# Retention with a convolution-gated unit: two float32 buffers behind those of the first two double chunks, value weights loaded later, first gated units held back a phase

## The chip, the core and the metric

The kernel runs on one core of a Trainium2 chip. The metric is the device time of a run in microseconds (us). One execution of the kernel was also recorded by the hardware profiler; its page and its trace are what the readings below come from. Engines are called as in the profile: PE is the matmul engine and PEld its weight loads, DVE, ACT and POOL are the vector, scalar and GpSimd engines, SP is the engine whose queue issues most DMAs.

## The reference

Inputs are q, k and v of shape (8 batches, 8 heads, 576 tokens, 64), and three weights: `w_val` (512 x 512), `conv_w` (5 x 512) and `w_out` (512 x 512). All are float32.

```python
scores = q @ k.T / sqrt(64)
gamma  = 1 - 2 ** (-5 - head)
D      = where(i >= j, gamma ** (i - j), 0)         # per head
x      = (scores * D) @ v                           # heads side by side: (8, 576, 512)
gate   = sigmoid(sum_k conv_w[k] * x[t - 4 + k])    # causal, per channel
out    = (gate * (x @ w_val)) @ w_out               # float32 (8, 576, 512)
```

## The kernel before

The 576 tokens of a batch are cut into two "double chunks" of 256 tokens and a tail of 64. The tails of four batches make one double chunk together. So there are 18 double chunks, m = 0 to 17; m = 8 and m = 17 are the tails. A double chunk has 0.5 MB each of q, k and v.

For one double chunk the work is as follows. SP loads q, k and v as float32 into tiles `fq`, `fk` and `fv` (`load`, L87; for a tail four smaller DMAs each, L92). POOL casts k and q to bf16 (`cast_k`, `cast_q`, L225) and multiplies v by powers of gamma (`cast_v`, L241). PE transposes k and q (`turn(0, m)` and `turn(1, m)`, L263), and ACT copies the result out of PSUM to `kq` (`take_turned`, L271). PE makes the scores (`scores`), DVE masks them (`masks`, L294), and PE multiplies by v (`values`, L308). A running state per batch carries what earlier chunks contribute: PE adds to it (`update`), ACT copies it out (`take_state`, L378), and PE applies it (`carried`). DVE scales the result into the bf16 tile x (`take_x`, L343), and POOL copies the last four tokens to the next chunk's tile (`pass_on`, L356).

The gated unit of a double chunk follows a turn later. The convolution is 40 matmuls with diagonal weights `dg` (`conv`), made on the chip from `conv_w` by `prep_conv_weights` and `prep_diagonals`. ACT applies the sigmoid (`gate`, L407). PE multiplies x by the value weights `wvb`, and DVE multiplies by the gate (`value`, L414 and L417; two calls, i = 0 and 1). Another turn later PE multiplies by the output weights `wob`, ACT copies the result to a tile `ob`, and SP stores it (`project`, L424, L432, L434; two calls).

The value weights arrive as float32 (`wvf`, L112) and are cast to `wvb` in two parts by `prep_wv` (L216), one part on POOL and one on ACT; `value(n, 1)` reads the part of POOL and `value(n, 0)` that of ACT. The output weights arrive as bf16 through POOL's own DMA queue (`load_wo`, L127).

The order is written out by hand: each engine executes its instructions in program order, and so does each queue. A prologue deals with m = 0 and begins m = 1 and 2. The main loop then takes m = 1 to 18. Turn m holds the scores and values of m, the convolution of m-1, `value` of m-1, `project` of m-2, the transposes of m+1, and the casts of m+2. `keep_warm` issues matmuls on zeros.

Tiles come from pools with a fixed number of buffers. The float32 tiles have LB = 4 buffers per kind, so a load of m waits until the cast of m-4 has read its buffer. `ob` has five buffers, so an eviction waits until the output five earlier has been stored. PSUM has two spare banks (`g`) that the convolution, `value` and `project` share.

SP issues the loads in this order: m = 0 and 1, the value weights, m = 2 and 3. In the prologue m = 4, 5 and 6 follow. In the main loop the load of m+6 stands in the middle of turn m, directly after each cast of m+2, between the two outputs of that turn:

```python
            if ok(m + 2):
                for (name, f) in (("k", cast_k), ("q", cast_q), ("v", cast_v)):
                    f(m + 2)
                    if ok(m + 2 + LB):
                        load(name, m + 2 + LB)
```

Of the kernel before, what the change touches and what calls it, by code (L numbers as in the profile page):

```python
# [13 lines left out]
F32 = mybir.dt.float32  # L14
# [7 lines left out]
def kernel(  # L22
# [23 lines left out]
    LB = 4  # L46
# [33 lines left out]
    with tc.manual_schedule():  # L80
# [14 lines left out]
        def load(name, m):  # L95
            t = ld.tile([P, H, R, D], F32, name=f"f{name}")
            fetch(nc.sync, t, {"q": q, "k": k, "v": v}[name], m)
            loaded[name, m] = t
# [3 lines left out]
        for m in range(2):  # L102
            for name in "kqv":
                load(name, m)
# [3 lines left out]
        wv_dst = wvf.rearrange("p (op ob) n -> ob p op n", ob=2)  # L108

        def load_wv(eng, i):  # L110
            for ob in range(2):
                eng.dma_start(out=wv_dst[ob, half[i]], in_=wv_src[ob, i ^ ob])  # L112

        for i in range(2):
            load_wv(nc.sync, i)
        for m in range(2, LB):
            for name in "kqv":
                load(name, m)


        ORDER = ((0, 0, 1, 0), (HP, 0, 0, 1), (0, 2, 0, 0), (HP, 2, 1, 1))
        wob = consts.tile([P, NP, DM], BF16, name="wob")

        def load_wo():
            src = moe_w_out.rearrange("(pr ab hl p) n -> ab hl p pr n", pr=2, ab=2, hl=2)
            for (p0, blk, ab, hl) in ORDER:
                nc.gpsimd.dma_start(out=wob[p0:p0 + HP, blk:blk + 2, :], in_=src[ab, hl])  # L127
# [9 lines left out]
        nc.vector.tensor_tensor(idb, ident[:, 0:HP], ident[:, HP:P], op=ALU.add)  # L137
        toki = consts.tile([P, NCH + 1, R], mybir.dt.int32, name="toki")
# [47 lines left out]
        identf = consts.tile([32, 32], F32, name="identf")  # L186
        nc.vector.tensor_copy(identf, ident[0:32, 0:32])
        id2 = consts.tile([P, HP], F32, name="id2")
        nc.vector.tensor_copy(id2, idb)
# [200 lines left out]
        def conv(n):  # L390

            g = [ps_g.tile([P, 2, 2 * P], F32, name="g") for _ in range(2)][::-1]
            gps[n] = g
            gsb[n] = {}
            lists = [], []
            for pr in range(2):
                a, b = 2 * pr, 2 * pr + 1
                for kk in range(KC):
                    for bank, rows, blks in ((0, half[1], (b, a)), (1, half[0], (a, b))):
# [44 lines left out]
        def keep_warm(n):  # L444

            t = ps_o.tile([P, NP, R, HP], F32, name="o0").rearrange("p o r n -> p (o r n)")
            for _ in range(n):
                nc.tensor.matmul(t, zeros[:, 0:P], zeros, start=True, stop=True)


        keep_warm(8)
        cast_k(0, (v_copy, 4))
        bank = turn(0, 0)
        take_turned(0, 0, bank, (v_copy, 4))
        cast_q(0)
        prep_conv_weights()
        prep_diagonals(0, nc.vector)
# [7 lines left out]
        for m in range(LB, LB + 2):  # L465
            for name in "kqv":
                load(name, m)
        prep_wv(g_copy, 1)
        keep_warm(3)
# [8 lines left out]
        take_state(0, 0)  # L478
        keep_warm(1)
# [3 lines left out]
        prep_diagonals(1, nc.vector)  # L483
        prep_diagonals(2, nc.vector)
        bank = turn(0, 1)
        take_turned(0, 1, bank)
        bank = turn(1, 1)
# [18 lines left out]
        for m in range(1, ND + 1):  # L506
# [43 lines left out]
            if m == 1:  # L550
                prep_wv(s_copy, 0)
                value(0, 1)
# [22 lines left out]
            value(m - 1, 0)  # L575
            if m > 1:
                project(m - 2, 1)
# [31 lines left out]
```

## Time and profile before

| | |
|---|---|
| median of 7 runs | 171.41 us (169.49 to 175.1) |
| the profiled execution | 170.14 us, span 168.4 us, so 1.74 us outside the span |
| mean granted PE clock | 0.961 |
| PE busy | 145.6 us, 86% of the span |
| PEld busy | 107.5 us, 64% |
| DVE busy | 101.0 us, 60% |
| ACT busy | 91.5 us, 54% |
| POOL busy | 77.3 us, 46% |
| DMA | 39.81 MB, mean 236 GB/s |

The span runs from the first to the last instruction. Busy time is the sum of an engine's instructions; it is an average over stages that can have different limits. The page cuts the span in 40 equal slices of 4.21 us and gives a digit for each (9 is 90% busy or more); the row GB/s gives what the DMA engines moved in each slice. A line of waits names the waiting engine, tile and line, then what ended the wait, the total in us, how often, and the longest. A line of a timeline gives start, length, engine, line, operation and count. A stretch line gives the limits, the length, busy times with the number of instructions, the granted clock, the DMA share and GB/s.

### The profile page before, as it was taken

Reading aid. Unit: us, or ns where it says so; the run is one execution under the profiler, and the core shown is the slowest. Engines: PE = TensorE matmul, PEld = TensorE weight load, DVE = VectorE, ACT = ScalarE, POOL = GpSimd, SP = SyncE. Lnnn points to the kernel's source line nnn. Section 1 sums busy time; section 2 is a strip of 40 time slices with the busy share of each in tenths; the row PEclk is TensorE's granted clock in tenths of the full one; section 3 lists DMA queues with packets and bytes.
Section 4 is the critical chain, followed back from the end, with each engine's and each line's share of the span. In section 5 each row is a group of like instructions: output and inputs, shape, how many; then the busy total and the mean of one; then the engine's idle time right before and its main releaser. Section 6 shows DMA issues by size and latency. Waiting matters only on the chain.

```text
span 168.4 us, 7599 instructions
## 1 busy us (share of the span) xinstructions
PE 145.6 (86%) x3344; PEld 107.5 (64%) x3378; DVE 101.0 (60%) x189; ACT 91.5 (54%) x149; POOL 77.3 (46%) x87
## 2 busy tenths in 40 slices
PE   7776888689994939999979999999999999999870
PEld 2355777457672836777757677777778677776620
DVE  6586356457574443677447676676777677667221
ACT  4773655356572514766546575657666575652340
POOL 4384597787749054081970264463828260000000
PEclk9998589999999996999999999999999999999996
DMA  4999999999996789999999999999787111131134
GB/s 132 347 343 222 317 283 260 324 303 323 269 301 159 161 230 298 281 345 312 335 315 344 304 318 308 348 298 272 166 204 264 68 70 62 66 126 64 66 125 125
DMA packets 69055, 39.81 MB, mean 236 GB/s; under 512 B 14219, under 2 KB 63903, under 8 KB 69023
## 3 DMA queue, kind: packets, MB, share of 16 engines
q1 hardware_dynamic: 68256, 38.54, 77.7%
q0 software_dynamic: 576, 0.52, 1.9%
q8 instruction: 26, 0.43, 1.1%
q10 hardware_dynamic: 190, 0.27, 0.6%
q14 instruction: 7, 0.05, 0.1%
HBM read 30.42 MB, written 9.44 MB: 237 GB/s over the span
## 4 chain that ended last, share of the span: by engine, by line
PE 56%; DMA 16%; SPq 10%; POOL 8%; issue 5%; ACT 2%; DVE 1%; ACTq 0%; POOLq 0%
PE g L424 14%; PE g L414 13%; PE g L253 10%; DMA fv<-in_v_dram 9%; PE tps L263 7%; PE o L308 6%; DMA fq<-in_q_dram 5%; PE s L253 4%; SPq L87 4%; SPq L92 4%; POOL vb L241 3%; SPq L112 2%; PE st L253 2%; POOL kb L225 2%; DMA out_dram<-ob 2%
## 5 line engine op out<-in xcount | busy, mean ns | idle before, releaser
L294 DVE TENSOR_TENSOR p<-s,mask 128x512 bf16<-128x512 f32 x62 | 39.9, 686 | 25.2 <-PE s L253 25.1
L271 ACT COPY kq<-tps 128x1024 bf16<-128x1024 bf16 x34 | 34.6, 1018 | 13.1 <-PE tps L263 12.8
L424 PE MATMUL g<-wob,z 128*128 128x512 bf16 x111 | 35.4, 385 | 5.9 <-ACT ob L432 2.7
L432 ACT COPY ob<-g 128x512 f32<-128x512 f32 x34 | 19.9, 586 | 33.8 <-PE g L424 24.8
L241 POOL TENSOR_TENSOR vb<-fv,gin 128x1024 bf16<-128x1024 f32 x18 | 34.3, 1907 | 5.5 <-DMA fv<-in_v_dram 5.5
L414 PE MATMUL g<-x,wvb 128*128 128x256 bf16 x272 | 36.1, 277 | 0.2 <-ACT gate L407 0.2
L253 PE MATMUL g<-x,dg 64*64 64x256 bf16 x720 | 32.3, 282 | 3.7 <-ACT ob L432 2.8
L343 DVE TENSOR_TENSOR x<-o,gout 128x512 bf16<-128x512 f32 x32 | 22.1, 745 | 13.8 <-PE o L308 13.8
L414 PEld LDWEIGHTS <-wvb 128*128 128x128 bf16 x288 | 26.9, 99 | 3.5 <-issue 0.6
L417 DVE TENSOR_TENSOR z<-gate,g 128x512 bf16<-128x512 f32 x34 | 23.4, 687 | 9.0 <-PE g L414 8.0
L356 POOL COPY x<-x 128x16 bf16<-128x16 bf16 x16 | 3.2, 198 | 55.6 <-DVE x L343 55.6
L253 PEld LDWEIGHTS <-dg 64*64 64x64 bf16 x720 | 24.2, 110 | 6.6 <-issue 5.5
L407 ACT ACTIVATE gate<-g 128x512 f32<-128x512 f32 x36 | 21.3, 603 | 10.9 <-PE g L253 5.7
L424 PEld LDWEIGHTS <-z 128*128 128x128 bf16 x144 | 14.1, 98 | 14.6 <-issue 3.4
L225 POOL CAST qb<-fq 128x1024 bf16<-128x1024 f32 x18 | 18.8, 1044 | 5.0 <-DMA fq<-in_q_dram 4.9
L225 POOL CAST kb<-fk 128x1024 bf16<-128x1024 f32 x17 | 17.7, 1044 | 1.5 <-DMA fk<-in_k_dram 1.2
L253 PEld LDWEIGHTS <-kq 64*64 64x64 bf16 x576 | 12.0, 109 | 8.2 <-issue 8.2
L253 PE MATMUL s<-kq 64*64 64x128 bf16 (+1 forms) x560 | 16.5, 222 | 0.8 <-ACT kq L271 0.6
L253 PE MATMUL st<-vb,kb 64*64 64x64 bf16 x512 | 14.3, 197 | 1.6 <-ACT sd L378 1.3
L253 PEld LDWEIGHTS <-kb 64*64 64x64 bf16 x512 | 13.0, 113 | 3.1 <-issue 2.8
L378 ACT CAST sd<-st 128x256 bf16<-128x256 f32 x24 | 8.9, 370 | 9.2 <-PE g L253 6.6
L308 PEld LDWEIGHTS <-vb 64*64 64x64 bf16 x576 | 8.3, 107 | 7.0 <-issue 6.8
(67 smaller groups left out, 113.4 us busy)
## 6 DMA issues: line engine op xcount, KB each, us to landing
fk<-in_k_dram SPq DMA_DIRECT2D x16, 512.0 KB, 6.1
fq<-in_q_dram SPq DMA_DIRECT2D x16, 512.0 KB, 6.4
fv<-in_v_dram SPq DMA_DIRECT2D x16, 512.0 KB, 7.1
out_dram<-ob SPq DMA_DIRECT2D x32, 256.0 KB, 4.2
wvf<-in_moe_w_val_dram SPq DMA_DIRECT2D x4, 256.0 KB, 6.2
fk<-in_k_dram SPq DMA_DIRECT2D x8, 128.0 KB, 4.7
fq<-in_q_dram SPq DMA_DIRECT2D x8, 128.0 KB, 3.9
fv<-in_v_dram SPq DMA_DIRECT2D x8, 128.0 KB, 3.6
```

Source lines behind the costliest of these rows:

```text
L225: copy(t[:, o:o + n], src[:, o:o + n])
L241: eng.tensor_tensor(vbf[m][:, h:h + n], loaded["v", m][:, h:h + n], g[:, h:h + n].unsqueeze(3).to_broadcast([P, n, R, D]), op=ALU.mult)
L253: return lambda: nc.tensor.matmul(*a, skip_group_check=True, **kw)
L271: copy(kq[m][:, which, o:o + n], bank[:, o:o + n])
L294: nc.vector.tensor_tensor(p[:, :, 0:n], sps[m, r][i][:, :, 0:n], mask[dcs[m][0], r].unsqueeze(1).to_broadcast([P, NP, n]), op=ALU.mult)
L308: nc.tensor.matmul(o, start=key not in opened, stop=False, skip_group_check=True, **kw)
L343: nc.vector.tensor_tensor(xg[b // GB][c][:, b % GB, :, x0:x0 + P].rearrange("p o (n r) -> p o r n", r=R), ops[m, ab], gout[:, :, t0:t0 + P ...
L407: nc.scalar.activation(t, gps[n][i], AF.Sigmoid)
L414: nc.tensor.matmul(vps[:, j, :], lhsT=wvb[:, o, 2 * i + j, :], rhs=xs(n, slice(0, P), o, PAD), start=(j == 0 and o == 0), stop=(j == 1 and ...
L417: nc.vector.tensor_tensor(z, gsb[n][i], vps, op=ALU.mult)
L424: nc.tensor.matmul(o, lhsT=zsb[n, j // 2][:, j % 2, i * P:(i + 1) * P], rhs=wob[:, j, :], start=(j == 0), stop=(j == NP - 1))
L432: nc.scalar.copy(ob, o)
```

## The change

The float32 tiles get two sets of buffers: one of two buffers per kind that only m = 0 and 1 use (`fke`, `fqe`, `fve`), and one of two buffers per kind that m = 2 to 17 share. The total of four per kind stays. SP now loads m = 0, 1 and 2 first, then three quarters of the value weights in two DMAs, then m = 3; the last quarter is issued by ACT, between two state copies of the prologue. The load of m = 4 follows the casts of m = 2. In the main loop the load of m+4 stands at the end of turn m, behind the outputs of that turn.

The convolution weights are prepared at the very beginning, two of the four diagonals on POOL, the other two on DVE. The cast of the value weights on POOL and the load of the output weights come after the casts of m = 2; the output weights take three DMAs instead of four. Turn 1 has no `value`; turn 2 has the four of m = 0 and 1, with ACT's weight cast ahead of them; turn 3 has the two of m = 2 and the four projections of m = 0 and 1. From turn 4 on the order of gated units is as it was. Warming matmuls are placed anew. In the weights the order of the half blocks in a tile changes (`ORDER`, and the blocks that `conv` names).

```diff
-    LB = 4
+    LB = 2
...
-            t = ld.tile([P, H, R, D], F32, name=f"f{name}")
+            t = ld.tile([P, H, R, D], F32, name=f"f{name}" + ("e" if m < 2 else ""))
...
-        for m in range(2):
+        for m in range(3):
             for name in "kqv":
                 load(name, m)
...
-        def load_wv(eng, i):
-            for ob in range(2):
-                eng.dma_start(out=wv_dst[ob, half[i]], in_=wv_src[ob, i ^ ob])
-
-        for i in range(2):
-            load_wv(nc.sync, i)
-        for m in range(2, LB):
-            for name in "kqv":
-                load(name, m)
+        nc.sync.dma_start(out=wv_dst[0], in_=moe_w_val.rearrange("(op ob p) n -> ob p op n", ob=2, p=P)[0])
+        nc.sync.dma_start(out=wv_dst[1, half[0]], in_=wv_src[1, 1])
+
+        def load_wv_rest():
+            nc.scalar.dma_start(out=wv_dst[1, half[1]], in_=wv_src[1, 0])
+
+        for name in "kqv":
+            load(name, 3)
...
-            for (p0, blk, ab, hl) in ORDER:
-                nc.gpsimd.dma_start(out=wob[p0:p0 + HP, blk:blk + 2, :], in_=src[ab, hl])
+            nc.gpsimd.dma_start(out=wob[:, 0:2, :], in_=src[HP:HP + P])
+            for pr in range(2):
+                nc.gpsimd.dma_start(out=wob[:, 2 + pr, :], in_=src[:, pr].rearrange("(t p) m -> t p m", p=HP)[0::3])
...
-        keep_warm(8)
+        keep_warm(4)
+        prep_conv_weights()
+        keep_warm(4)
         cast_k(0, (v_copy, 4))
+        for o in range(2):
+            prep_diagonals(o, nc.gpsimd)
         bank = turn(0, 0)
         take_turned(0, 0, bank, (v_copy, 4))
         cast_q(0)
-        prep_conv_weights()
-        prep_diagonals(0, nc.vector)
+        prep_diagonals(2, nc.vector)
+        prep_diagonals(3, nc.vector)
...
-        for m in range(LB, LB + 2):
-            for name in "kqv":
-                load(name, m)
-        prep_wv(g_copy, 1)
-        keep_warm(3)
+        keep_warm(2)
...
         take_state(0, 0)
+        load_wv_rest()
         keep_warm(1)
...
-        prep_diagonals(1, nc.vector)
-        prep_diagonals(2, nc.vector)
         bank = turn(0, 1)
         take_turned(0, 1, bank)
+        keep_warm(2, spare(ps_g, "g"))
...
-        for (name, f) in (("k", cast_k), ("q", cast_q)):
+        keep_warm(4, spare(ps_g, "g"))
+        for (name, f) in (("k", cast_k), ("q", cast_q), ("v", cast_v)):
             f(2)
             load(name, LB + 2)
+        prep_wv(g_copy, 1)
         load_wo()
-        cast_v(2)
-        load("v", LB + 2)
-        prep_diagonals(3, nc.vector)
...
-            if m == 1:
-                prep_wv(s_copy, 0)
-                value(0, 1)
             if nxt:
                 bank = turn(0, m + 1)
                 take_turned(0, m + 1, bank)
-            if m > 1:
-                value(m - 1, 1)
-                project(m - 2, 0)
+
+            if m == 2:
+                prep_wv(s_copy, 0)
+            for (f, n, i) in {1: (), 2: ((value, 0, 1), (value, 0, 0)),
+                              3: ((value, 2, 1), (project, 0, 0), (project, 0, 1))}.get(
+                                  m, ((value, m - 1, 1), (project, m - 2, 0))):
+                f(n, i)
             if ok(m + 2):
-                for (name, f) in (("k", cast_k), ("q", cast_q), ("v", cast_v)):
-                    f(m + 2)
-                    if ok(m + 2 + LB):
-                        load(name, m + 2 + LB)
+                cast_k(m + 2)
+                cast_q(m + 2)
+                cast_v(m + 2)
...
-            value(m - 1, 0)
-            if m > 1:
-                project(m - 2, 1)
+            for (f, n, i) in {1: (), 2: ((value, 1, 1), (value, 1, 0)),
+                              3: ((value, 2, 0), (project, 1, 0), (project, 1, 1))}.get(
+                                  m, ((value, m - 1, 0), (project, m - 2, 1))):
+                f(n, i)
+            for name in "kqv":
+                if ok(m + 2 + LB):
+                    load(name, m + 2 + LB)
```

More of the change, by code (lines that the diff above doesn't have):

```diff
@@ L108 @@
         wv_dst = wvf.rearrange("p (op ob) n -> ob p op n", ob=2)
-        def load_wv(eng, i):
-            for ob in range(2):
-                eng.dma_start(out=wv_dst[ob, half[i]], in_=wv_src[ob, i ^ ob])
-        for i in range(2):
-            load_wv(nc.sync, i)
-        for m in range(2, LB):
-            for name in "kqv":
-                load(name, m)
-        ORDER = ((0, 0, 1, 0), (HP, 0, 0, 1), (0, 2, 0, 0), (HP, 2, 1, 1))
+        nc.sync.dma_start(out=wv_dst[0], in_=moe_w_val.rearrange("(op ob p) n -> ob p op n", ob=2, p=P)[0])
[4 more added lines that the diff above has]
+            load(name, 3)
+        ORDER = ((0, 0, 0, 1), (HP, 0, 1, 0), (0, 2, 0, 0), (HP, 2, 1, 1))
         wob = consts.tile([P, NP, DM], BF16, name="wob")
         def load_wo():
-            src = moe_w_out.rearrange("(pr ab hl p) n -> ab hl p pr n", pr=2, ab=2, hl=2)
-            for (p0, blk, ab, hl) in ORDER:
-                nc.gpsimd.dma_start(out=wob[p0:p0 + HP, blk:blk + 2, :], in_=src[ab, hl])
+            src = moe_w_out.rearrange("(pr n) m -> n pr m", n=2 * P)
+            nc.gpsimd.dma_start(out=wob[:, 0:2, :], in_=src[HP:HP + P])
+            for pr in range(2):
+                nc.gpsimd.dma_start(out=wob[:, 2 + pr, :], in_=src[:, pr].rearrange("(t p) m -> t p m", p=HP)[0::3])
         zeros = consts.tile([P, DM], BF16, name="zeros")
@@ L137 @@
         nc.vector.tensor_tensor(idb, ident[:, 0:HP], ident[:, HP:P], op=ALU.add)
+        identf = consts.tile([32, 32], F32, name="identf")
+        nc.vector.tensor_copy(identf, ident[0:32, 0:32])
+        id2 = consts.tile([P, HP], F32, name="id2")
+        nc.vector.tensor_copy(id2, idb)
         toki = consts.tile([P, NCH + 1, R], mybir.dt.int32, name="toki")
@@ L185 @@
         warm = consts.tile([P, 1], F32, name="warm")
[L186 to L189, printed above, removed]
         xg = [[xp.tile([P, GB, NP, PAD + (W if c < NCH else TAIL)], BF16, name=f"x{g}{c}") for c in range(NCH + 1)]
@@ L398, in conv @@
                 for kk in range(KC):
-                    for bank, rows, blks in ((0, half[1], (b, a)), (1, half[0], (a, b))):
+                    for bank, rows, blks in ((0, half[1], (a, b)), (1, half[0], (a, b))):
                         lists[bank].append([mm(g[bank][half[i], pr, :], lhsT=dg[rows, blks[i], kk, :],
@@ L442, with keep_warm @@
         v_copy, g_copy, s_copy = nc.vector.tensor_copy, nc.gpsimd.tensor_copy, nc.scalar.copy
-        def keep_warm(n):
-            t = ps_o.tile([P, NP, R, HP], F32, name="o0").rearrange("p o r n -> p (o r n)")
+        def keep_warm(n, t=None):
+            if t is None:
+                t = ps_o.tile([P, NP, R, HP], F32, name="o0").rearrange("p o r n -> p (o r n)")
             for _ in range(n):
                 nc.tensor.matmul(t, zeros[:, 0:P], zeros, start=True, stop=True)
-        keep_warm(8)
+        keep_warm(4)
+        prep_conv_weights()
+        keep_warm(4)
         cast_k(0, (v_copy, 4))
+        for o in range(2):
+            prep_diagonals(o, nc.gpsimd)
         bank = turn(0, 0)
```

## The prediction

> **What bounds the kernel now.** I read the page first (busy tenths, then the chain), then the table of stretches with one stretch per turn of the main loop, then the timelines of PE, POOL and the SP queue up to 75 us, and last the waits of the stretch that is out of line. A turn m begins at its first score matmuls.
>
> ```profile
> PE   7776888689994939999979999999999999999870
> GB/s 132 347 343 222 317 283 260 324 303 323 269 301 159 161 230 298 281 345 312 335 315 344 304 318 308 348 298 272 166 204 264 68 70 62 66 126 64 66 125 125
> ```
>
> PE is full from slice 15 (63 us) on; before that there are holes, and the DMA runs near 300 GB/s with a dip to 160 in slices 12 and 13. The stretches of turns 1 to 6, and turn 13 for comparison (columns: length, PE, PEld, DVE, ACT, POOL busy, granted clock, DMA share, GB/s):
>
> ```profile
> 14.85:25.24 10.39, 8.80 (x185) 7.40 (x185) 6.00 (x11) 4.79 (x8) 6.43 (x10) 0.67 1.07 285
> 25.24:34.89 9.65, 7.74 (x182) 5.64 (x184) 5.78 (x9) 4.35 (x7) 7.17 (x7) 1.00 1.12 285
> 34.89:43.32 8.43, 7.68 (x192) 5.70 (x194) 5.34 (x8) 4.94 (x8) 6.37 (x8) 1.00 1.10 322
> 43.32:51.41 8.09, 7.63 (x199) 5.89 (x200) 5.33 (x8) 5.10 (x9) 4.78 (x5) 1.00 0.99 284
> 51.41:65.02 13.61, 8.34 (x192) 5.82 (x194) 5.33 (x9) 4.62 (x8) 7.24 (x7) 0.93 0.74 185
> 65.02:72.99 7.97, 7.87 (x183) 6.20 (x185) 5.33 (x8) 4.82 (x8) 0.87 (x3) 0.91 1.03 307
> ...
> 119.48:126.92 7.44, 7.33 (x186) 5.68 (x192) 5.64 (x9) 4.82 (x8) 4.12 (x5) 1.00 0.80 201
> ```
>
> 7.44 us is what a turn costs when PE alone sets it (7.33 busy). Turn 5 takes 13.61, and turns 1 to 3 exceed 7.44 too, although turn 1 projects nothing. The waits of 51 to 66 us, and the SP queue of that time:
>
> ```profile
> ACT ob L432 <- DMA out_dram<-ob: 7.9, 2, 4.6
> ...
> 35.57 1.40 SPq L87 DMA_DIRECT2D fk<-in_k_dram  x1
> ...
> 46.28 1.83 SPq L434 DMA_DIRECT2D out_dram<-ob  x1
> 48.21 2.96 SPq L92 DMA_DIRECT2D fk<-in_k_dram  x4
> 51.26 4.61 SPq L92 DMA_DIRECT2D fq<-in_q_dram  x4
> 55.97 3.66 SPq L92 DMA_DIRECT2D fv<-in_v_dram  x4
> 59.73 1.04 SPq L434 DMA_DIRECT2D out_dram<-ob  x2
> ```
>
> The outputs issued at 59.73 were evicted by ACT at 35.0 and 40.5. They stood behind six prefetched full loads (35.57 to 44.74) and twelve tail loads, because a load of m+6 comes in program order ahead of the outputs of turns that PE finished long ago. With five `ob` buffers ACT could not evict, so PE stood: this is the 6 us hole of turn 5.
>
> **What the Trainium skill says.** "DMA: Bandwidth & Descriptors", section "Queues, rings and completion order": on each DMA engine descriptors of a row are consumed in ring order, and the engine alternates between rows that have work. So an output issued on SP waits for SP's earlier loads, and ACT's or POOL's DMA does not. The trace agrees for SP (59.73 above). The same page, "Specifications", puts line rate at transfers of 512 B or more: full loads have 512 B runs and make 300 to 345 GB/s, tail loads 256 B runs and 159 to 161. "TensorE: Matmul & The Clock Gate", section "Part 1: The HAM clock gate": the array starts throttled and activity frees it. The trace agrees in turn 1: granted clock 0.67, conv matmuls 0.42 us instead of 0.27.
>
> **Part 1: two buffers behind the first two; loads at a turn's end.** Nothing is added on an engine: the same 54 loads of q, k and v. Load m+4 is now issued at the end of turn m, after that turn's outputs, where before load m+6 was in turn m's middle. It waits for the cast of m+2. In steady turns POOL casts directly after `pass_on`, some 7 us into the turn before (`pass_on(6)` at 72.14, casts of m=9 until 76.2, which is 3 us into turn 7), so that buffer is free before the load's place in SP's order. The load lands about 6 us after issue (issue table 6.1 to 7.1), that is 14 us after turn m began, just when POOL comes to cast m+4 (7.44 + 7); the cast takes 4 us, until 18. The first user is `update(m+4)` or `turn(0, m+4)` in turn m+3, at 3×7.44 + 2.7 = 25 us. That leaves 7 us of slack. The DMA has 1.57 MB of loads and 0.52 MB of outputs per turn: 2.10 MB / 7.44 us = 282 GB/s, below the 314 to 329 seen in turns 7 to 11. The tail chunk takes about 10 us at 160 GB/s plus 1.6 us for outputs, so it eats some 4 us of the slack once and not all of it. I therefore cost the shallower prefetch at nothing; the cover is those 7 us. If it were gone, each us of lateness would stop PE through `kb`/`vb`.
>
> What goes: in turn 5 outputs no longer have tail loads for m=8 issued in front of them from turn 2. The tail loads now come after turn 4's outputs, the outputs of turn 5 behind them, and the five `ob` buffers cover two and a half turns, 18 us, against 10 for the tail. So turn 5: 13.61 → 7.5 (−6.1); turn 4: 8.09 → 7.6 (−0.5); turn 6, which starts with the echo and clock 0.91: 7.97 → 7.5 (−0.5). Sum −7.1. Next late there is PE itself.
>
> **Part 2: order of the first transfers.** Value weights stood before m=2 (4 DMAs, 1.05 MB, about 3.3 us at 320 GB/s; slice 3, when they ran with 64 partitions each, made only 222). Before, `kb` of m=2 began at 19.66 waiting for its load. Now it can land near 14 to 15 us, and the cast follows `pass_on(0)` at about 16. One quarter of the weights goes out on ACT between two state copies; an ACT issue of 0.63 us (`cwn`) fits the 0.53 us idle plus a 0.2 us gap there; bounds 0 and +0.9 (if it takes the 1.45 of a blocked SP issue); I take +0.1. On POOL the weight casts (2, 1.17 together) and the output-weight DMAs (3 instead of 4, 0.63 each) now come after vb of m=2 and ahead of kb of m=3: q and v of m=2 landing near 16 and 17.4, vb is done at about 20.2, and 20.2 + 1.2 + 1.9 = 23.3, then kb until 24.4. `turn(0,3)` wants it at about 26: hidden, by 1.6 us.
>
> **Part 3: prologue.** `cw` and the diagonals move to the front. DVE: three small copies, 0.50, now before the first kb cast (was waiting 0.28 for its load): +0.25, if `cwn` has landed by 4.2 us. Its landing is not in the trace; bounds 0 and +1.0; I take +0.3. Two diagonals on POOL: no POOL row of 320 elements; vb takes 1.90 for 1024, so 0.6 each as an estimate, 1.2 in a 3.66 us wait for fq. DVE loses 0.88 and 0.48 later, beside PE work. One warming matmul goes before the first scores and six come later: two lie in the 1.1 us that PE waits for ACT; four of 0.26 to 0.40 stand before the scores of turn 1: 14.43 + 1.3, so scores at 15.6 instead of 14.85; the conv was waiting for x until 15.7 anyway. Start of turn 1: +0.75 in all, the +0.1 and +0.3 lying beneath (the chain there goes through vb, which waits for fv at 7.88).
>
> **Part 4: gated units held back.** Turn 1 loses two values (1.89 and 1.04) and the ACT cast of 1.14; turn 2 has four values and no projection; turn 3 two values, four projections. After that the work is level again. Turn 1 becomes a chain: scores 0.5, conv 1.4, updates with sd 0.9, scores 0.45, masks 1.3, values and carried 0.9, turn and its ACT copy 1.7, handovers 0.25: 7.4; if the clock falls as before (0.67) up to 1.3 more; I take 7.9. Turn 2: 7.44 − 2×0.97 + 2×0.87 = 7.24, plus 1.2 for `value(0,0)` behind ACT's casts, plus 0.7 for sd and copies: 9.1. Turn 3: 7.44 + 1.94 + the 0.65 of stalls it had: 10.0. Turn 4 thus begins at 15.6 + 7.9 + 9.1 + 10.0 = 42.6, before 43.32: −0.7. Bounds: −4 if PE has hardly a stall, +2 if the clock stays low or a weight is late. The relabelled blocks of the weights cost nothing: same tiles and counts of matmuls.
>
> **Sum.** −0.7 − 7.1 = −7.8. Span 168.4 → 160.6, and with the 1.74 outside the span 170.14 → 162.3 us. The median shown (171.41) is 1.3 above the profiled run; I take its disturbance to be the DMA backlog, which goes.
>
> **Rivals.** *A, the outputs still queue (0.12):* turn 3 now makes four outputs and the tail still has 12 slow DMAs ahead of turn 5's. For: by 66 us nine chunks, the weights and eight outputs must have moved (14.15 + 1.57 + 2.10 = 17.8 MB), where before 16.7 MB had moved by 63 (the first 15 slices of GB/s times 4.21 us). Against: better-shaped weight DMAs and the 18 us of `ob`. Half of turn 5's hole stays, at a later turn: 162.3 + 3.5 = 165.8. *B, two buffers starve the loop (0.10), the slower side:* with only one chunk in flight, the queue runs empty between a landing, a cast and the next issue. The place is POOL's wait for fk/fv in turns 7 to 14. It decides from below 282 GB/s; at 245 a turn takes 8.56, and about nine turns lose 1.1 each: 162.3 + 10.1 = 172.4. For: the DMA is 90% used at 6.7 us per chunk (SP's k issues at 74.08, 80.93, 86.85, 93.55, 100.93). Against: the slack of 7 us, and that those loads ran no more than four or five ahead. *C, it doesn't speed up the beginning but delays it (0.08):* late wob or a cold clock, turns 1 to 3 at +2: 165.0.
>
> **Numbers.** Forecast 0.70, A 0.12, B 0.10, C 0.08. Range 159.5 (the start at −3.5 instead of −0.7) to 167.5 (A with the colder half of C). A measurement of this kernel can tell about 1%. Faster by over 1%: 0.86, within 1% 0.05, slower 0.09.
>
> **What would show it.** Right: no wait of ACT for out_dram; turn 5 at 7.5; turns 7 to 14 at 7.44 to 7.7 with load landings near 6 us; turn 4 starting at 41 to 44. Wrong: POOL waiting for fv beyond turn 4 with PE idle (B), a new ob wait after the tail (A), turn 1 above 9 us or clock under 0.7 in turn 2 (C).

## The result and the profile after

The changed kernel takes 168.89 us (median of 24 runs, 166.57 to 171.39) against 170.7 us (61 runs, 167.24 to 175.31) for the kernel before. The ratio is 0.992, 95% interval [0.9885, 0.9958]: 0.8% faster, where 4.6% were forecast. A second measurement gave 0.994 [0.9887, 0.9999]. The ratio compares the faster runs of both kernels, since each has some executions that are a few per cent slower; so it is not the quotient of the two medians. The direction was right, the size was not.

The profiled execution of the changed kernel took 170.03 us (span 168.1), a little above its median, and that of before 170.14 (span 168.4), a little below its own. So the two profiles differ by less than the medians do; what follows is the account of these two executions.

From the page of the changed kernel (40 slices of 4.20 us):

```profile
PE   6987748688999999999869997999699999999970
PEclk9999996999999999999999999999999999999999
GB/s 124 347 347 315 301 303 224 264 160 198 266 366 293 331 177 187 287 301 293 327 348 304 254 271 230 288 213 279 299 309 153 162 174 209 64 129 63 65 125 125
...
q0 software_dynamic: 2352, 0.53, 2.5%
...
q8 instruction: 26, 0.43, 1.1%
```

PE is now full from slice 10 on, where it was full from slice 15, but the row of nines has gaps at slices 20, 24 and 28. The slices 6 to 9 move little, and the queue of the output weights (q0) has 2352 packets where it had 576. The table of stretches, turns 1 to 6 and then turns 9, 11 and 13 (columns as before: PE, PEld, DVE, ACT, POOL busy, granted clock, DMA share, GB/s):

```profile
15.65:22.44 6.79, 4.66 (x169) 3.93 (x169) 4.28 (x7) 3.77 (x6) 4.07 (x4) 1.00 1.15 300
22.44:34.80 12.36, 9.20 (x193) 7.37 (x193) 5.94 (x9) 4.80 (x8) 8.71 (x10) 0.86 1.08 255
34.80:45.87 11.07, 9.83 (x212) 6.66 (x215) 5.94 (x9) 5.61 (x10) 6.20 (x6) 1.00 0.74 198
45.87:53.77 7.90, 7.44 (x198) 5.70 (x194) 5.35 (x8) 5.01 (x9) 5.13 (x6) 1.00 1.04 331
53.77:61.68 7.91, 7.62 (x191) 5.70 (x193) 5.34 (x9) 4.83 (x8) 4.36 (x5) 1.00 0.97 272
61.68:69.17 7.49, 7.38 (x184) 5.60 (x186) 5.37 (x9) 4.83 (x8) 1.91 (x2) 1.00 0.81 200
...
84.60:93.71 9.11, 7.55 (x183) 5.61 (x184) 5.34 (x9) 4.93 (x8) 4.99 (x6) 1.00 1.08 328
101.15:110.00 8.85, 7.53 (x184) 5.63 (x185) 5.34 (x9) 4.93 (x8) 4.23 (x5) 1.00 0.91 264
117.44:126.44 9.00, 7.40 (x183) 5.60 (x184) 5.33 (x9) 4.93 (x8) 4.23 (x5) 1.00 0.99 303
```

The hole of turn 5 is gone (13.61 to 7.91), and no wait of ACT for a store is left. Turn 2 has grown from 9.65 to 12.36, and three later turns cost 9 us instead of 7.44. The timeline of PE shows what stood there (the bracket is the idle time ahead of the group and what ended it; "issue" is a wait for nothing that the profile records):

```profile
24.48 1.49 PE L252 MATMUL g<-x,dg 64*64 64x256 bf16 x24 [1.40 <-issue]
30.84 1.05 PE L413 MATMUL g<-x,wvb 128*128 128x256 bf16 x8 [1.32 <-ACT wvb L215]
40.60 1.24 PE L423 MATMUL g<-wob,z 128*128 128x512 bf16 x5 [0.39 <-DMA wob<-in_moe_w_out_dram]
82.07 0.31 PE L307 MATMUL o<-kq,sl 64*64 64x64 bf16 x14 [0.62 <-issue]
88.10 0.41 PE L252 MATMUL s<-kq 64*64 64x128 bf16 x14 [1.45 <-issue]
104.50 0.30 PE L252 MATMUL s<-kq 64*64 64x128 bf16 x7 [1.21 <-issue]
121.18 0.62 PE L262 MATMUL tps<-ident,kb 128*128 128x128 bf16 x8 [1.49 <-issue]
```

The sum of the four late "issue" waits is 4.77 us. Before had one in that time:

```profile
86.60 0.26 PE L308 MATMUL o<-kq,sl 64*64 64x64 bf16 x9 [1.11 <-issue]
```

The beginnings of turns (first score matmul) in us, for the kernels that the text compares most. The last column but one is the length of turns 7 to 16, which have the same work in all; "forecast" is the prediction's own sum.

| kernel | turn 1 | turn 2 | turn 3 | turn 4 | turn 7 | turn 17 | 7 to 16 | span |
|---|---|---|---|---|---|---|---|---|
| before | 14.85 | 25.24 | 34.89 | 43.51 | 72.99 | 149.18 | 76.19 | 168.4 |
| forecast | 15.6 | 23.5 | 32.6 | 42.6 | 65.2 | 141.4 | 76.2 | 160.6 |
| changed | 15.58 | 22.44 | 34.80 | 45.87 | 69.17 | 148.77 | 79.60 | 168.1 |
| changed, again | 16.65 | 24.09 | 36.46 | 47.12 | 70.15 | 148.66 | 78.51 | 168.0 |
| buffer part alone | 14.80 | 25.17 | 37.45 | 46.06 | 69.56 | 146.46 | 76.90 | 165.7 |
| buffer part, again | 14.83 | 24.45 | 35.00 | 43.61 | 67.47 | 144.97 | 77.50 | 164.2 |
| start alone | 15.31 | 23.36 | 34.20 | 45.17 | 78.73 | 153.82 | 75.09 | 173.2 |
| buffer part, projections held back | 14.76 | 25.50 | 33.71 | 44.15 | 67.04 | 144.74 | 77.70 | 164.0 |
| POOL's new order and longer program | 16.50 | 25.00 | 34.23 | 44.89 | 67.77 | 143.34 | 75.57 | 162.7 |
| changed, no loads from m = 9 | 15.30 | 22.45 | 35.99 | 46.65 | 70.56 | 144.74 | 74.18 | 163.9 |

Against the forecast the changed kernel loses 3.3 us in turns 1 to 3 (30.29 instead of 27.0), 0.7 in turns 4 to 6 (23.30 instead of 22.6), and 3.4 in turns 7 to 16: 7.4 of the 7.5 us missing.

### The profile page after: what moved, and what is told of

Read it like the earlier page. It is cut to its first block, busy times and chain, and to the rows that moved or that the text cites. A ratio compares the mean times of both kernels' runs of the same rounds, so it can differ in the third digit from the quotient of the medians.

```text
span 168.1 us, 7603 instructions
## 1 busy us (share of the span) xinstructions
PE 145.4 (87%) x3350; PEld 106.5 (63%) x3383; DVE 100.2 (60%) x187; ACT 91.9 (55%) x149; POOL 80.3 (48%) x88
## 3 DMA queue, kind: packets, MB, share of 16 engines
q0 software_dynamic: 2352, 0.53, 2.5%
## 4 chain that ended last, share of the span: by engine, by line
PE 67%; DMA 14%; SPq 7%; issue 5%; ACT 2%; POOL 2%; DVE 1%; ACTq 0%
PE g L423 17%; PE g L413 15%; PE g L252 11%; PE tps L262 9%; DMA wob<-in_moe_w_out_dram 9%; PE o L307 7%; SPq L87 7%; DMA wvf<-in_moe_w_val_dram 5%; PE s L252 5%; PE st L252 2%; PE s L413 1%; ACT ob L431 1%; POOL wvb L215 1%; POOL wob L124 1%; DVE ob L429 1%
## 5 line engine op out<-in xcount | busy, mean ns | idle before, releaser
L240 POOL TENSOR_TENSOR vb<-fv,gin 128x1024 bf16<-128x1024 f32 x16 | 30.5, 1905 | 16.1 <-DMA fv<-in_v_dram 16.0
L423 PE MATMUL g<-wob,z 128*128 128x512 bf16 x113 | 34.8, 379 | 2.0 <-DMA wob<-in_moe_w_out_dram 0.4
L413 PE MATMUL g<-x,wvb 128*128 128x256 bf16 x272 | 35.1, 272 | 1.6 <-ACT wvb L215 1.3
L252 PEld LDWEIGHTS <-dg 64*64 64x64 bf16 x720 | 23.5, 107 | 5.7 <-issue 4.6
L224 POOL CAST qb<-fq 128x1024 bf16<-128x1024 f32 x16 | 16.7, 1045 | 12.5 <-DMA fq<-in_q_dram 7.8
L224 POOL CAST kb<-fk 128x1024 bf16<-128x1024 f32 x16 | 16.7, 1045 | 6.9 <-DMA fk<-in_k_dram 2.4
L252 PEld LDWEIGHTS <-kq 64*64 64x64 bf16 x576 | 11.8, 108 | 11.2 <-issue 10.7
L252 PEld LDWEIGHTS <-kb 64*64 64x64 bf16 x512 | 12.5, 112 | 3.0 <-issue 2.8
```

What stands on the lines that cost most here:

```text
L224: copy(t[:, o:o + n], src[:, o:o + n])
L240: eng.tensor_tensor(vbf[m][:, h:h + n], loaded["v", m][:, h:h + n], g[:, h:h + n].unsqueeze(3).to_broadcast([P, n, R, D]), op=ALU.mult)
L252: return lambda: nc.tensor.matmul(*a, skip_group_check=True, **kw)
L413: nc.tensor.matmul(vps[:, j, :], lhsT=wvb[:, o, 2 * i + j, :], rhs=xs(n, slice(0, P), o, PAD), start=(j == 0 and o == 0), stop=(j == 1 and ...
L423: nc.tensor.matmul(o, lhsT=zsb[n, j // 2][:, j % 2, i * P:(i + 1) * P], rhs=wob[:, j, :], start=(j == 0), stop=(j == NP - 1))
```

## The experiments

### The two halves of the change

The buffer part alone (edit on the kernel before):

```diff
-    LB = 4
+    LB = 2
-            t = ld.tile([P, H, R, D], F32, name=f"f{name}")
+            t = ld.tile([P, H, R, D], F32, name=f"f{name}" + ("e" if m < 2 else ""))
-        for m in range(LB, LB + 2):
-            for name in "kqv":
-                load(name, m)
...
-                    if ok(m + 2 + LB):
-                        load(name, m + 2 + LB)
...
+            for name in "kqv":
+                if ok(m + 2 + LB):
+                    load(name, m + 2 + LB)
```

> The kernel before with the buffer part alone: two buffers for m = 0 and 1 and two for the rest, load m+4 at a turn's end; start, weights and gated units as before. Theory 1 (the buffers remove turn 5's hole, the changed start loses it again): no wait of ACT for a store, turns 5 and 6 at 7.5 us, so 3 to 5 us faster than before. Theory 2 (two buffers cost what they bring, by keeping the DMA behind for longer): within 1 us of before.

165.75 us; ratio 0.9757 [0.9703, 0.9812]. One wait of ACT for a store was left, of 0.7 us. Theory 1 holds in the main: the buffer part is worth 2.4%, more than the whole change. Turns 4 to 6 take 23.5 us against 29.5, though turn 5 took 8.15 and not 7.5. (A repetition follows below.)

The start alone (edit on the changed kernel: `LB = 4`, one set of names, loads of m+6 behind the casts as before):

> The changed kernel with four shared buffers again and load m+6 in the middle of turn m: only the new start, weights and held-back gated units remain. Theory 1: the store hole of about 6 us is back, and turns 1 to 3 are no shorter than before, so 0 to 3 us slower than before. Theory 2: the start is worth 1 to 2 us by itself.

176.46 us; ratio 1.0381 [1.0318, 1.0443], slower by 6.4 us, more than either theory allowed. Turns 1 to 3 are no shorter, and the hole is deeper than before:

```profile
49.58 4.00 SPq L92 DMA_DIRECT2D fk<-in_k_dram  x4
53.67 2.63 SPq L92 DMA_DIRECT2D fq<-in_q_dram  x4
56.40 2.63 SPq L92 DMA_DIRECT2D fv<-in_v_dram  x4
59.13 1.04 SPq L433 DMA_DIRECT2D out_dram<-ob  x2
...
62.84 1.91 PE L252 MATMUL g<-x,dg 64*64 64x256 bf16 x30 [8.66 <-ACT ob L431]
```

Two projections of m = 0 have become two of the four in turn 3, so no output at all comes ahead of the tail loads on SP, where before there was one (46.28). All five `ob` buffers fill, and PE waits 8.66 us. The reading of the hole that the prediction gave is shown from both sides: the same queue order with later outputs makes it longer, the other queue order takes it away.

### The waits without a cause

In the listing of PE's program the matmuls at which PE stood in the changed kernel are instructions 702, 3258, 3514, 4280 and 5046 (the number counts the matmuls and weight loads ahead of the first not issued, within one pair). The distances are 2556, 256, 766 and 766. PE's program has 21 further instructions, such as waits. Counted with these, the places are 708, 3267, 3524, 4292 and 5060, and all distances are multiples of 256 (10, 1, 3 and 3) to within one instruction. The one wait of before, at 86.60 us, is at 3258 of its own program, in the same part of the tail's turn. The profile's page counts 26 DMAs of instructions with 0.43 MB, and 26×256 is 6656, about the length of PE's program (6766 matmuls and weight loads). The Trainium skill, "Runtime: NRT & Kernel Launch", section "Instruction fetch mechanics", says that an engine's program is brought in blocks of 16 KiB, 256 instructions, by a DMA queue of its own, and that the crossing is "mostly hidden". By count that holds here: of some 26 crossings five show a wait above 0.5 us in the changed kernel.

PE's program made longer at the start:

```diff
-        keep_warm(4)
+        t = ps_o.tile([P, NP, R, HP], F32, name="o0").rearrange("p o r n -> p (o r n)")
+        for _ in range(48):
+            nc.tensor.matmul(t[:, 0:32], zeros[:, 0:P], zeros[:, 0:32], start=True, stop=True)
```

> The changed kernel with four of the warming matmuls at the start replaced by 48 small ones, so that PE's program is 88 instructions longer ahead of the loop. PE stood without a recorded cause at its instructions 702, 3514, 4280 and 5046 of the program, a spacing of whole blocks of 255.6. Theory F (PE waits for the next block of its own instructions): the stalls lie at the same counts, so 88 instructions (44 matmuls) earlier in the work: not in the scores and transposes of turns 9, 11 and 13 but in the convolution and state updates ahead of them. Rival (the stalls belong to the work there, to a semaphore or a memory bank): they stay at the same matmuls.

```profile
80.78 0.81 PE L413 MATMUL g<-x,wvb 128*128 128x256 bf16 x6 [0.74 <-issue]
117.31 0.41 PE L252 MATMUL g<-x,dg 64*64 64x256 bf16 x8 [0.74 <-issue]
```

Both waits that are left stand at 3258 and 5046 of the new listing, 44 matmuls earlier in the work: a value matmul of turn 8 and the convolution of turn 13, where the changed kernel did not wait. At 702, 3514 and 4280 no wait is recorded this time. With the program's other instructions counted, the two places are 3267 and 5059, 7×256 apart. So the waits belong to the count, not to the work, though not every block brings one. (166.96 us in its one execution.)

Without the stores of double chunks 4 to 14:

```diff
+            if 4 <= n < 15:
+                return
             if kind == "full":
                 nc.sync.dma_start(out=out[u, ...
```

> The changed kernel without the stores of double chunks 4 to 14 (that part of the output is left out), so that the DMA has a quarter less to move per turn. Theory F (the blocks of PE's instructions come late because the DMA engines are full): the stalls without a cause at about 86, 103 and 120 us vanish or fall under 0.4 us each, the turns 9, 11 and 13 take 7.44 to 7.6 us instead of 8.9 to 9.1, and the span falls by about 4 us. Rival (a stall at a block's end doesn't depend on the DMA): they stay.

The waits after 66 us sum to 0.4 us; the one at 702, which comes before any of these stores, is 1.67. 166.35 us in one execution. In favour of F, but a quarter less traffic is a weak lever, and another kernel with all its traffic showed as little (0.4, below). So the DMA was emptied:

```diff
+            if m >= 9:
+                loaded[name, m] = loaded[name, m % 2]
+                return
             t = ld.tile(...)
```

> The changed kernel without the loads of double chunks 9 to 17 (their casts read the tiles of m = 0 and 1, so the output of these chunks is not the reference's). Theory F (the blocks of PE's program come late because the DMA engines are full): with the DMA nearly empty from turn 6 on, no wait without a cause above 0.2 us in turns 8 to 16, every full turn 7.44 us; the wait of 1.4 us in turn 2 stays. Rival: the waits at 3514, 4280 and 5046 stay.

```profile
78.01:85.17 7.16, 7.05 (x191) 5.33 (x192) 4.17 (x8) 4.45 (x7) 7.11 (x6) 1.00 0.22 78
85.17:92.64 7.47, 7.36 (x183) 5.57 (x184) 5.33 (x9) 4.82 (x8) 0.85 (x2) 1.00 0.19 74
92.64:100.09 7.45, 7.34 (x192) 5.71 (x194) 5.33 (x9) 4.82 (x8) 3.92 (x5) 1.00 0.24 68
100.09:107.53 7.44, 7.33 (x184) 5.60 (x185) 5.33 (x8) 4.83 (x8) 4.13 (x5) 1.00 0.28 79
```

The last such wait is 0.79 us at 57.07, in turn 5, and turns 7 to 16 take 74.18 us: 5.4 less than in the changed kernel, 2.0 less than before. Turn 2 still has its wait (1.24). The longer program and the emptied DMA together show that PE waits for the next block of its own program (a block wait, from here on), and that in these runs it does so only while the DMA engines are busy with loads. A full DMA does not always bring a wait: the start alone moved 348 GB/s in turn 9 (93.52 to 101.33 us) and PE stood 0.15 us. But the measurement goes beyond the skill's words in size: where a crossing was not hidden, it cost up to 3.08 us (at 3514, in the kernel with the old prologue below):

```profile
88.41 0.35 PE L251 MATMUL s<-kq 64*64 64x128 bf16 x9 [3.08 <-issue]
```

The sum of these waits after 66 us varies from kernel to kernel and execution to execution: before 1.1, changed 4.8 and 3.6, buffer part 1.3 and 2.5, start alone 0.3, the kernels below between 0.4 and 5.7. What of it belongs to a kernel and what to chance is not settled.

The changed kernel and the buffer part once more:

> The changed kernel once more, beside the next three on one chip, for a second profile of it. If its late start is its own (theory S), turn 2 is again above 11 us and turn 4 begins at 45 us or later; if PE's waits without a cause in turns 8 to 13 (4.8 us in the first profile, 1.1 before) belong to the change (theory F), they are again above 3 us; if they are chance, they are 1 to 2 us as in the other kernels.

> The buffer part alone once more, on the chip of these, for comparison: 2 to 3% faster than before, waits without a cause in turns 8 to 13 of 1 to 2 us in all (1.3 in its first profile).

Changed: 168.64 us, ratio 0.9943 [0.9887, 0.9999], with turn 2 at 12.37 us, turn 4 at 47.12, and 3.6 us of waits. So the late start was there both times. Buffer part: 167.16 us, ratio 0.9777 [0.9635, 0.9919]; its profile had 164.2 us of span, and turn 4 began at 43.61 where it had begun at 46.06.

### What makes the start late

Output weights in four DMAs, as in the kernel before:

> The changed kernel with the output weights in four DMAs of 64 partitions x 2 x 512 in place of three. Theory W (the last two of the three, which landed 12.3 and 14.9 us after issue and go with 1776 more packets on that queue, hold the DMA at 160 to 260 GB/s from 25 to 42 us): the weights land in 5 to 8 us, the slices of that time go back to about 300 GB/s, about 1 to 2 us faster than the changed kernel. Rival (PE waited for the weights only 0.4 us, and the DMA lag is covered): no change beyond 0.5 us.

167.71 us; ratio 0.9887 [0.9848, 0.9925] against 0.9921 [0.9885, 0.9958] for three: no difference that can be told. The packets of q0 go back to 576 (2352 before this edit), the slices from 29 to 42 us reach 276 to 339 GB/s, and PE no longer waits for these weights. So two of the three DMAs, of the odd shape, really were slow (12.3 and 14.9 us to landing), and covered but for 0.39 us: the rival was right.

In addition ACT's cast of the value weights at the end of turn 1:

```diff
-            if m == 2:
-                prep_wv(s_copy, 0)
...
                 take_turned(1, m + 1, bank)
+            if m == 1:
+                prep_wv(s_copy, 0)
```

> The one before this, and ACT's cast of the value weights moved from the middle of turn 2 to the end of turn 1, where ACT was idle. Theory (the 1.3 us that PE stood for value(0,0) in turn 2 is on the path): turn 2 shorter by 1.0 to 1.3 us, and the time too. Rival (the weights land at 21 us, too near to the cast, so ACT's state copies and gates of turn 2 come later): no gain.

166.27 us; ratio 0.9707 [0.9626, 0.9788]. The wait for `wvb` in turn 2 is gone, but turn 2 took 12.80 us in its profile:

```profile
24.00:36.80 12.80, 11.67 (x192) 8.95 (x191) 6.01 (x9) 4.71 (x8) 10.06 (x12) 0.61 1.09 279
```

PE is busy for 11.67 us with work that took 7.99 in the start alone, at a clock of 1.00. The time fell and turn 2 grew, so a second measurement follows:

> The version with four output-weight DMAs and ACT's weight cast in turn 1 once more, beside the one above: its ratio was 0.971 in one measurement and its descendants had 0.980 to 0.987. If the first value was a lucky draw it comes to 0.98, with turn 2 again cold and above 11 us.

168.61 us; ratio 0.9897 [0.9832, 0.9961], turn 2 at 12.57 us with clock 0.73. The first ratio was not repeated, and no gain of this edit can be claimed. The two intervals don't even overlap, so a difference of 1 to 2% between versions that were measured once each is not safe in this document.

Eight more warming matmuls in turn 1:

> The version with four output-weight DMAs and ACT's weight cast in turn 1, and eight more warming matmuls in the idle places of turn 1 (three after the transposes of k, five after those of q). Theory S (in that version turn 2 ran at a clock of 0.61 and PE was busy for 11.7 us with work that takes 7.5 at full clock): turn 2 at a clock above 0.9 and at most 10 us, 2 to 3 us faster than the version without. Rival (the clock falls for another reason, or the eight matmuls cost what they bring): no gain.

166.81 us; ratio 0.9865 [0.9789, 0.9940]. Turn 2 takes 11.45 us at clock 0.85. Half of what was expected of the profile, and nothing of the time. PE stood 1.62 us at the same instruction 702 (16 instructions earlier in the work, for the eight matmuls; the profile puts this wait down to DVE's mask, which the waiting convolution does not read), and the cold matmuls (0.42 us each) come after that. Warming in turn 1 did not help, since the idle place is in turn 2; that this is why the clock fell is likely and not shown.

The prologue of before on that version:

> The version with four output-weight DMAs and ACT's weight cast in turn 1, but with the prologue of the kernel before (convolution weights and diagonals later, warming matmuls as before). Theory: the new prologue is worth at most 0.5 us by its order, but its six later warming matmuls keep the clock up in turn 1; without them turn 1 runs at a clock near 0.7 and takes 1 us more, so 0.5 to 1.5 us slower than the version with it. Rival: no difference, since turn 2 is cold in both.

168.17 us; ratio 0.9890 [0.9781, 1.0000], inside the spread of the version's own two ratios. Its profile (span 169.4) has 5.7 us of block waits after 66 us, so it can't be read for the prologue. Inconclusive.

Held-back gated units on the buffer part, all else as before:

```diff
             if m == 1:
                 prep_wv(s_copy, 0)
-                value(0, 1)
...
-            if m > 1:
-                value(m - 1, 1)
-                project(m - 2, 0)
+            for (f, n, i) in {1: (), 2: ((value, 0, 1), (value, 0, 0)),
+                              3: ((value, 2, 1), (project, 0, 0), (project, 0, 1))}.get(
+                                  m, ((value, m - 1, 1), (project, m - 2, 0))):
+                f(n, i)
```

The second half of the turn is edited likewise, with the lists of the change.

> The buffer part alone (2.4% faster than before) and, of the start, only the held-back gated units; weights, first loads and prologue as before, ACT's weight cast in turn 1. Theory S (holding back takes matmuls out of turn 1, PE idles there and its clock is low in turn 2, so nothing is won): turn 1 about 7.5 us, turn 2 at a clock under 0.8 and above 10 us, the time within 1% of the buffer part alone. Rival (holding back saves the wait for the output weights in turn 2): 1 to 2 us faster than the buffer part alone.

166.96 us; ratio 0.9833 [0.9779, 0.9886], 0.8% above the buffer part. Turn 1 takes 10.48 us at clock 0.53 and turn 2 9.47 at 0.80: turn 1 does not get shorter (PE waits 0.75 us for `kb` of m = 2, whose load here comes after the weights), and it is cold. Theory S holds for the time, but turn 2 was to be above 10 us and under 0.8: the coldest turn is the first.

POOL's order in the version with ACT's cast in turn 1:

```diff
-        prep_wv(g_copy, 1)
-        load_wo()
+        cast_k(3)
+        prep_wv(g_copy, 1)
+        cast_q(3)
+        load_wo()
```

> On the version with four output-weight DMAs and ACT's weight cast in turn 1: POOL casts k of m=3 ahead of the value weights and q of m=3 ahead of the output weights. Theory K (POOL's order makes kb of m=3 late, 27.5 to 28.7 us, because it stands behind weights that land at 23 to 24 us; turn 2 waits for it, and PE's wait of 1.4 to 1.6 us at its instruction 702 only lies over it): kb of m=3 done by 25 us, but the wait at 702 stays, so turn 2 shorter by at most 1 us. Rival (the wait at 702 alone sets turn 2): no change in turn 2.

> The one before this with PE's program 88 instructions longer at the start, so that block 702 ends in turn 1 and not at turn 2's convolution. Theory K with F (two waits lie over each other, and only taking both away helps): no wait above 0.5 us in turn 2's convolution and none for kb, turn 2 at most 10 us, 2 us or more faster than the version with POOL's new order alone. Rival (turn 2 is long because its clock is low, whatever the waits): turn 2 still above 11 us.

POOL's order alone: 166.33 us, ratio 0.9816 [0.9728, 0.9904]. k of m = 3 is cast by 24.8 us instead of 27.5 in the changed kernel, the wait at 702 stays (0.78), and turn 2 still takes 13.02 us, at clock 0.61. With the longer program as well: 165.2 us, ratio 0.9805 [0.9733, 0.9876], and the stretches of turns 1 and 2:

```profile
16.50:25.00 8.50, 4.79 (x169) 3.94 (x169) 4.34 (x7) 3.82 (x7) 4.58 (x5) 0.96 1.06 266
25.00:34.23 9.23, 8.79 (x193) 7.70 (x192) 5.93 (x9) 4.75 (x8) 9.23 (x13) 0.86 1.11 283
```

Turn 2 now takes 9.2 us, against 9.1 in the forecast; the block wait (1.50 us) has moved into turn 1. Both turns together are 17.7 us, against 20.5 with POOL's order alone and 19.2 in the changed kernel. In the ratio the two versions can't be told apart. That POOL's cast had been a wait behind the wait was seen in the kernel with only the longer program, where the block ends in turn 1 too:

```profile
28.73 1.03 PE L262 MATMUL tps<-ident,kb 128*128 128x128 bf16 x8 [2.62 <-POOL kb L224]
```

The start alone, above, has the same start as the changed kernel, and shows the same from the other side:

```profile
23.36:34.20 10.84, 7.99 (x192) 6.34 (x191) 5.93 (x9) 4.80 (x8) 9.00 (x10) 1.00 1.09 260
...
27.43 0.62 PE L262 MATMUL tps<-ident,kb 128*128 128x128 bf16 x8 [1.05 <-POOL kb L224]
```

Here PE did not stand at 702 and the clock stayed at 1.00; turn 2 took 10.84 us, with 1.05 of waiting for `kb`, which the changed kernel does not show. So three things lie over each other in turn 2: the late cast of k, the block wait, and the low clock. Taking one away brings out the next, and in the changed kernel the block wait and the clock together lengthened the turn by 1.5 us (12.36 − 10.84), less than the block wait and its cold matmuls add up to. These are single executions, and such starts differ by 1 to 2.5 us from one to the next. What makes the clock fall was not isolated.

Only the projections held back, on the buffer part:

```diff
-                project(m - 2, 0)
+                for n, i in {2: (), 3: ((0, 0), (0, 1))}.get(m, ((m - 2, 0),)):
+                    project(n, i)
...
-            if m > 1:
-                project(m - 2, 1)
+            for n, i in {1: (), 2: (), 3: ((1, 0), (1, 1))}.get(m, ((m - 2, 1),)):
+                project(n, i)
```

> The buffer part alone (ratio 0.976 and 0.978 in two measurements) with the projections of m = 0 and 1 held back to turn 3 and the values where they were, so that turn 2 doesn't wait for the output weights (1.56 and 1.24 us in the two profiles of the buffer part) and turn 1 keeps its matmuls. Theory: no wait for the output weights, turn 2 at most 9 us, turn 3 about 10, together 1 to 2 us less, ratio about 0.970. Rival (turn 2 without projections idles and its clock falls, as it did when the values were held back): ratio 0.976 or above.

165.37 us; ratio 0.9757 [0.9697, 0.9818]. Turn 2 takes 8.21 us at full clock, turn 3 10.4, and the wait for the output weights is gone, as the theory said; but turn 4 begins at 44.15, in the range of the buffer part (43.61 and 46.06), and the ratio is the same. Miss: no gain of 0.5% is seen. The buffer part alone and this version have the lowest ratios here that a second measurement did not take back, 2.4% under the kernel before; the ratio of the buffer part was measured twice, that of this version once.

## Why the prediction was right or wrong

**What bounds the kernel (right).** The hole of turn 5 came from outputs behind prefetched loads in SP's order. The two halves show it. (What the trace shows at 59.73 is the order of issue on SP; what happens after issue, which the cited page is about, no run here separates.) Turns 4 to 6 went from 29.48 to 23.30 us; the forecast had 22.6, and the difference lies in turns 4 and 5, at 7.9 each where 7.6 and 7.5 were set. The prediction's row for turn 4 begins 0.19 us before the first score matmul (43.51). From there turn 4 took 7.90 us before as after, so the 0.5 us that it was to gain were not there.

**Part 1, two buffers cost nothing (right for q, k and v, wrong in what it left out).** POOL waits for its loads longer (`vb` for `fv` 16.0 us in all, 5.5 before), and none of that reached PE: turns without a block wait took 7.44 to 7.5. Rival B (starved loop) did not occur. The first step that failed is the price of turns 7 to 16, carried over from before with nothing added: "I therefore cost the shallower prefetch at nothing; the cover is those 7 us" counted only q, k and v. These turns took 3.4 us longer (2.3 in the second profile). What the working left out is that the same full DMA also carries PE's program: the block waits rose from 1.1 us before to 4.8 and 3.6. The row "q8 instruction" and the wait of 1.11 us at 86.60 stood in the profile of before, and the prediction did not ask what the 8.65 us of turn 8 was. Whether the change itself makes these waits longer stays open: with four buffers they were 1.1 and 0.3 us, with two between 0.4 and 5.7.

**Part 2, weights behind three double chunks (wrong).** "vb is done at about 20.2, and 20.2 + 1.2 + 1.9 = 23.3, then kb until 24.4 ... hidden, by 1.6 us". vb was done at 21.05, 0.85 later; the last of the weights landed only at 22.6 (issued at 14.03, 8.6 to landing), so POOL idled and its cast began at 22.77 (the profile names no cause for this wait, but it ends 0.15 us after the landing); and the three DMAs took POOL 2.55 us instead of 1.9:

```profile
22.77 1.17 POOL L215 CAST wvb<-wvf 128x512 bf16<-128x512 f32 x2 [1.72 <-issue]
...
26.38 1.08 POOL L224 CAST kb<-fk 128x1024 bf16<-128x1024 f32 x1
```

`kb` of m = 3 was done at 27.46, 3 us later than worked out. The turn wanted it at about 26; PE, held by the block wait, came to it at 28.0, so the lateness was hidden here by luck, and showed in the start alone (1.05 us). The largest term that was mis-sized is the landing of the weights: it was left out of the sum. For the transfers of q, k and v the working held: k of m = 2 was cast at 16.18 without waiting for its load.

**Part 3 (right in size).** Turn 1 began at 15.58, forecast 15.6. `cwn` made PE wait 0.24 us, the two diagonals on POOL took 1.87 us instead of 1.2, and both lay in POOL's wait for q, whose cast began at 6.43 instead of 6.28.

**Part 4 (wrong).** Turn 1 took 6.9 instead of 7.9 us, better than forecast. Turn 2 took 12.36 instead of 9.1. By the rows above: PE busy 9.20 us, 1.40 of block wait, 1.32 for `wvb`, 0.44 for a state copy; together 12.36. The busy time is 2.07 more than the 7.13 of the working (7.33 − 1.94 + 1.74). Not all of that is the clock: at 0.86 it can have cost at most 1.7 us of this turn (0.14 × 12.36), and the start alone, at 1.00, still had 7.99. So the estimate is some 1.2 us for the clock and 0.9 for work that the sum put too low. The forecast had the wait for `wvb` (1.2), 0.7 for state copies, and nothing for clock or block. The clock was considered for turn 1 and in rival C, at +2 in all and a chance of 0.08; in the profiles of versions with this start PE was busy in turn 2 for 7.99 us (start alone, clock 1.00) to 11.8 (clock 0.61). Turn 3 took 11.07 instead of 10.0, 0.56 of it more PE work than the 9.27 worked out, 0.39 the output weights.

**The sum.** −0.7 − 7.1 was forecast for the profiled execution; it was +2.4 for the start of turn 4, −6.2 for turns 4 to 6, +3.4 for turns 7 to 16, +0.1 after. Rival C was nearest in its cause, but it had only the start, at 2.7 us over the forecast where it was 3.3, and not the 3.4 us of turns 7 to 16; and it was rated too low. That the kernel got faster at all is due to the buffer part. Which piece of the new start costs the 1.6% between the buffer part and the whole change is not settled.

## What to carry to other kernels

A store that stands behind prefetched loads in one queue holds its buffer as long as those loads take: put the load behind the stores of its turn, and count buffers from the last store that got out. Taking matmuls out of a thin warm-up turn need not shorten the path when what follows waits for the same transfers, and it can cost clock: with the gated units alone held back, turn 1 took 10.48 us at 0.53, against 10.37 and 9.62 at 0.84 and 1.00 in the buffer part. "Issue" waits at distances of 256 instructions were here the engine's own program arriving late. To see their price, compare with a kernel whose DMA is empty, and look for them before a turn's time is carried into a forecast.

## What the runs showed of the hardware that was not expected

PE waited for blocks of its program for up to 3.08 us each, at distances of whole multiples of 256 instructions, in turns in which the DMA engines moved 264 to 328 GB/s (changed kernel), and not at all when they moved 68 to 79.

Two DMAs of 128 partitions whose source steps over 64-row blocks (128 KB each, as the page counts them) landed 12.3 and 14.9 us after issue, where the four DMAs of 64 partitions landed in 5.3 to 7.3 us before and 5.6 to 7.0 in the changed start. The data were not cut smaller: in both cases they went in 512 packets of 1 KB. The 1776 packets more on that queue are of 4 bytes each. Why they are sent, and whether they or something else makes these DMAs slow, is open.

The prologue and turns 1 and 2 differ from execution to execution by 1 to 2.5 us: in two profiles of the buffer part turn 4 began at 46.06 and 43.61 us, with a granted clock of 0.84 and 0.86 in turns 1 and 2 of the one, and 1.00 in both of the other.
